# Lightning attention, LayerNorm and MLP on one core: 64-token chunks for two more pairs, block products for two more groups, and a newly written order of the steady part

## The chip, the cores and the metric

The kernel runs on one core of one Trainium2 chip. A core has a matrix engine (TensorE, PE in the profile; its weight loads are a row of their own, PEld), a vector engine (VectorE, DVE), an activation engine (ScalarE, ACT), a general engine (GpSimd, POOL) and a sync engine (SyncE, SP) that here only issues DMAs. The engines run side by side and wait for each other on semaphores. The metric is device time in microseconds (us) of one execution.

## The reference

Inputs are q, k and v of shape (4 batches, 8 heads, 768 tokens, 64), a decay `lam` per head, a gain of 512 and two weight matrices (512 x 2048 and 2048 x 512), all float32. The core of what is computed:

```python
for b in range(nb):                       # 12 blocks of 64 tokens, one after the other
    qb, kb, vb = q[:, :, sl], k[:, :, sl], v[:, :, sl]
    intra = (qb @ kb^T) * Dmask           # Dmask[i,j] = lam^(i-j) for i >= j, else 0
    intra = intra @ vb
    inter = (qb * lam^(pos+1)) @ kv_state
    out[:, :, sl] = intra + inter
    kv_state = lam^64 * kv_state + (kb * lam^(63-pos))^T @ vb
x = out as (4, 768, 512)                  # heads side by side
mu, var = mean and variance of x over the last axis
xn = (x - mu) / sqrt(var + 1e-6) * g_ln
result = x + maximum(xn @ w_ch1, 0) @ w_ch2
```

The state makes one sequence of a batch sequential; a chunk of 128 tokens in place of 64 gives the same result with other decays.

## The kernel before

**Tiling.** The work is cut into 12 pairs u = 0 to 11. A pair is 256 tokens of one batch (u counts batches first, then the three stretches of 256 tokens), that is two tiles of 128 tokens. Each pair goes through: load of k, q and v (256 tokens x 8 heads x 64 each, 512 KB); casts to bf16 with the decay folded into q and v (`in_k`, `in_q`, `in_v`, on GpSimd, VectorE or ScalarE); a transposition of k and q into `kqT` (on TensorE for pairs 0 to 2, by two DMAs, `transpose_dma` in L253, for pairs 3 to 10, by one for pair 11); scores, mask, scores times v (`av`), the state's update (`kv`, `new_state`) and its contribution (`inter`); then LayerNorm (`norm`, `rstd_of`), a transposition of the normalised rows into `xT` (`to_xT`, on TensorE for pairs 0 to 4, by two DMAs for the others), layer 1 of the MLP with a relu into `hT`, and layer 2, with the residual added as the accumulators are emptied.

**Two forms of attention.** Pairs u < LB = 6 work in chunks of 128 tokens: `scores` (L266) makes 128-wide products, `av` (L427) takes 64 small matmuls. Pairs from LB on work in chunks of 64: `scores64` (L361), `av64` (L416, 32 matmuls), `kv64`, and `states64`, which forms two states per tile on VectorE and GpSimd. The form also decides the shape of the loads: `fill` (L72) fetches a tensor of a pair below LB in one DMA whose rows are 512 bytes, and of a pair from LB on in two DMAs with rows of 256 bytes.

**Two forms of layer 2.** Groups g are pairs again. Groups 0 to 3 use the dense form `m2` (L667): per tile 16 matmuls of 128x512 into one accumulator. Groups 4 to 11 use seven block products (`product`, `m2w`): the hidden and output dimensions are halved, operand sums of `hT` are formed on VectorE (`h_sums`, L557), combinations of the weights are formed once (`w_sums`, L802), and each product is 8 matmuls of 128x256. Its seven results are scaled and added up by `evict` (L587) on VectorE, ScalarE and GpSimd.

**What sets the order.** Nothing is scheduled: every engine runs its instructions in the order in which the Python code issues them. The steady part is a hand-written list of statements; `units(n)` issues the next n pieces of MLP work from a second list, `plan`, and functions such as `X(u)` and `s12(u)` issue several attention steps. All loads of k, q and v, all DMA transpositions and all stores stand in one queue, SP's, in the order of the list; the loads of w1 and w2 stand in GpSimd's. The input buffers are three deep per tensor, accumulators for MLP work four (tag mm), for attention's output one per tile (po0, po1), for scores two (sc).

Of the kernel before, what the change touches and what calls it, by code (L numbers as in the profile page):

```python
# [17 lines left out]
def kernel(  # L18
# [436 lines left out]
    def reader(u):  # L455
        s = st[u]
        for ab in range(2):
            if s["S"][ab][1] is not None:
# [53 lines left out]

    def rstd_of(u):
        s = st[u]
        std = wk.tile([128, 2], F32, tag="std", name="std")
        if "sum" in s:
            ss = xp.tile([128, 2], F32, tag="ss", name="ss")
            for ab in range(2):
                sq = wk.tile([128, DM], BF16, tag="sq", bufs=1, name="sq")
                nc.scalar.activation(sq, s["x"][:, ab], ACT.Square, bias=s["nmean"][:, ab:ab + 1], accum_out=ss[:, ab:ab + 1])  # L520
            nc.scalar.activation(std, ss, ACT.Sqrt, bias=eps_t, scale=XS * XS / DM)
# [869 lines left out]
```

## Time and profile before

| | before |
|---|---|
| median of 3 runs | 207.53 us (207.52 to 208.06) |
| span of the profiled execution (first to last instruction) | 205.7 us |
| TensorE busy | 195.9 us, 95% |
| VectorE busy | 133.4 us, 65% |
| ScalarE busy | 122.0 us, 59% |
| GpSimd busy | 83.9 us, 41% |
| moved by DMA | 36.41 MB in 91011 packets |
| layer 1 matmuls (L547), 640 | 73.9 us busy |
| dense layer 2 matmuls (L684), 128 | 29.8 us busy |

The profile is that of one execution. A row of the page's fifth part, or of the view that groups instructions, reads: line of the kernel, engine, operation, output<-input by the program's names, shape, count | busy time in us, mean of one in ns | idle time of the engine ahead of them and what ended it. In the chain of waits each row has a start, a duration and a group of instructions. A row of SP's queue gives the start of an issue and the time until the queue was free for the next one; when the transfer itself has landed is told by the view of DMA issues. Durations of single matmuls overlap (a mean of 273 ns stands beside a rate of one in 109 ns), so rates are taken from the chain.

### The profile page before, as it was taken

The page shows a single profiled execution, that of the slowest core. Times are in us where ns is not written, and L with a number is a line of the kernel's source. Part 1 is how long each engine was busy: PE and PEld are TensorE (multiplying, and loading weights), DVE is VectorE, ACT ScalarE, POOL GpSimd, SP SyncE. Part 2 cuts the span into 40 slices and gives each one's busy share as a digit, 9 for nine tenths or more (in the row PEclk, how much of TensorE's full clock was granted, in tenths as well). Part 3 has the DMA queues.
Part 4 walks back from the last instruction along what each step waited for, and adds up shares of the span by engine and source line. Part 5 has one row for each costly group of instructions (what it writes and reads, how often), then busy time and mean ns, then how long its engine had stood idle before and what let it go on. Part 6 is the DMA issues. An engine that isn't in the chain of part 4 may idle for free.

```text
span 205.7 us, 7488 instructions
## 1 busy us (share of the span) xinstructions
PE 195.9 (95%) x3223; PEld 157.8 (77%) x3223; DVE 133.4 (65%) x277; ACT 122.0 (59%) x281; POOL 83.9 (41%) x117
## 2 busy tenths in 40 slices
PE   1997999999999999999999999999999999999992
PEld 0485798545784686489889888888888888988881
DVE  3588352626766458777889774857877947865253
ACT  3787678535357468166575775585586565652630
POOL 5557039317656341464273261772273202002020
PEclk9999999999999999999999999999999999999999
DMA  3999999999899998999799999887988020178404
GB/s 105 301 255 203 179 281 192 198 293 277 194 268 252 217 183 190 170 256 213 165 201 134 220 213 135 207 169 128 234 133 183 4 51 3 26 131 273 139 7 97
DMA packets 91011, 36.41 MB, mean 177 GB/s; under 512 B 65121, under 2 KB 88161, under 8 KB 90978
## 3 DMA queue, kind: packets, MB, share of 16 engines
q1 hardware_dynamic: 86368, 31.53, 74.9%
q0 software_dynamic: 4224, 4.19, 12.7%
q8 instruction: 25, 0.41, 0.9%
q10 hardware_dynamic: 386, 0.20, 0.4%
q14 instruction: 8, 0.07, 0.1%
HBM read 27.27 MB, written 6.29 MB: 163 GB/s over the span
## 4 chain that ended last, share of the span: by engine, by line
PE 85%; DMA 6%; DVE 2%; ACT 2%; SPq 1%; issue 1%; POOL 0%; POOLq 0%; DVEq 0%
PE pm L547 34%; PE pm L684 14%; PE pm1t L658 6%; PE pwd L582 6%; PE pwa L582 6%; PE pwc L582 6%; DMA w<-in_moe_w_ch_dram 4%; PE pwb L582 3%; DMA qin<-in_q_dram 3%; PE po L449 2%; PE po L436 2%; DVE x L595 1%; PE po L423 1%; PE sc L370 1%; PE sc L279 1%; PE pk L324 1%
## 5 line engine op out<-in xcount | busy, mean ns | idle before, releaser
L547 PE MATMUL pm<-xT,w 128*128 128x256 bf16 x640 | 73.9, 273 | 0.4 <-DMA w<-in_moe_w_ch_dram 0.4
L547 PEld LDWEIGHTS <-w 128*128 128x128 bf16 x640 | 61.2, 98 | 8.7 <-DMA w<-in_moe_w_ch_dram 0.5
L550 ACT ACTIVATE hT<-pm 128x512 f16<-128x512 f32 x80 | 47.1, 597 | 28.7 <-PE pm L547 28.5
L684 PE MATMUL pm<-w,hT 128*128 128x512 f16 x128 | 29.8, 380 | 0.0
L582 PEld LDWEIGHTS <-hs 128*128 128x128 f16 x256 | 24.9, 98 | 2.9
L607 POOL TENSOR_TENSOR x<-ev_u,x 128x256 f32<-128x256 f32 x8 | 5.9, 743 | 48.8 <-ACT ev_u L606 37.4
L330 POOL TENSOR_TENSOR Sn<-Stmp,lam_s 128x256 bf16<-128x256 f32 x16 | 9.8, 616 | 33.0 <-DVE Stmp L408 17.9
L565 DVE TENSOR_TENSOR hs<-hT 128x1024 f16<-128x1024 f16 x16 | 12.7, 795 | 15.8 <-ACT hT L550 14.5
L684 PEld LDWEIGHTS <-hT 128*128 128x128 f16 x128 | 11.8, 98 | 12.4
L582 PEld LDWEIGHTS <-hT 128*128 128x128 f16 x192 | 18.7, 98 | 2.1
L658 PE MATMUL pm1t<-xT,w 128*128 128x128 bf16 x256 | 15.6, 219 | 1.0 <-DMA w<-in_moe_w_ch_dram 0.7
L477 DVE SCALAR_TENSOR_TENSOR xc<-po,nmean,g_row 128x512 bf16<-128x512 f32 x18 | 13.0, 745 | 5.0 <-ACT nmean L476 4.9
L658 PEld LDWEIGHTS <-w 128*128 128x128 bf16 x256 | 14.8, 98 | 1.5 <-DMA w<-in_moe_w_ch_dram 0.8
L475 ACT ACTIVATE x<-po 128x512 f32<-128x512 f32 x18 | 10.6, 590 | 7.8 <-PE po L449 4.5
L242 POOL TENSOR_TENSOR vb<-vin,lam_v 128x1024 bf16<-128x1024 f32 (+1 forms) x7 | 11.6, 1659 | 4.8 <-DMA vin<-in_v_dram 4.7
L520 ACT ACTIVATE sq<-x,nmean 128x512 bf16<-128x512 f32 x18 | 12.9, 719 | 0.3
L242 POOL TENSOR_TENSOR vb<-vin,lam_p 128x1024 bf16<-128x1024 f32 x6 | 11.4, 1896 | 3.1 <-ACT hT L550 1.9
L289 DVE TENSOR_TENSOR mA<-sc,keep 128x512 bf16<-128x512 f32 x14 | 9.0, 682 | 4.9 <-PE sc L279 4.9
L661 ACT ACTIVATE hT<-pm1t 128x512 f16<-128x512 f32 x16 | 9.6, 598 | 4.4 <-PE pm1t L658 4.3
L595 DVE SCALAR_TENSOR_TENSOR x<-pwd,rstd,x 128x256 f32<-128x256 f32 x16 | 7.7, 481 | 3.4 <-POOL x L615 3.4
L595 DVE SCALAR_TENSOR_TENSOR x<-pwa,rstd,x 128x512 f32<-128x512 f32 (+1 forms) x16 | 9.1, 612 | 0.8
L582 PE MATMUL pwa<-w,hT 128*128 128x256 f16 x64 | 9.6, 273 | 0.0
(137 smaller groups left out, 318.0 us busy)
## 6 DMA issues: line engine op xcount, KB each, us to landing
out_dram<-x SPq DMA_DIRECT2D x22, 256.0 KB, 4.0
w<-in_moe_w_ch_dram POOLq DMA_DIRECT2D x8, 512.0 KB, 8.0
kin<-in_k_dram SPq DMA_DIRECT2D x14, 256.0 KB, 5.2
qin<-in_q_dram SPq DMA_DIRECT2D x14, 256.0 KB, 4.2
vin<-in_v_dram SPq DMA_DIRECT2D x14, 256.0 KB, 5.3
kin<-in_k_dram SPq DMA_DIRECT2D x5, 512.0 KB, 6.2
qin<-in_q_dram SPq DMA_DIRECT2D x5, 512.0 KB, 7.0
vin<-in_v_dram SPq DMA_DIRECT2D x5, 512.0 KB, 6.1
```

The costliest lines, as they stand in the source:

```text
L242: eng.tensor_tensor(st[u]["vb"][:, hs], qkv_in[u]["v"][:, hs], lv.to_broadcast([128, n, 2, D]), op=ALU.mult)
L330: eng.tensor_tensor(dst, src, lam_s[:, :, None].to_broadcast([128, NP, D]), op=ALU.mult)
L475: nc.scalar.activation(x, po, ACT.Copy, accum_out=sm)
L477: nc.vector.scalar_tensor_tensor(xc, in0=po, scalar=nm, in1=g_row, op0=ALU.add, op1=ALU.mult)
L520: nc.scalar.activation(sq, s["x"][:, ab], ACT.Square, bias=s["nmean"][:, ab:ab + 1], accum_out=ss[:, ab:ab + 1])
L547: nc.tensor.matmul(pm[:, b, :], lhsT=w1[n // W2K][:, kk, (n % W2K) * 128:(n % W2K + 1) * 128], rhs=xT_of[g][:, kk, 0:N], start=(b == 0 and ...
L550: nc.scalar.activation(hT[:, u * NB:(u + 1) * NB, 0:N], pm, ACT.Relu)
L565: nc.vector.tensor_tensor(s13, b[:, :, 1:2, :].to_broadcast([128, n, 2, 128]), b[:, :, 0:4:3, :], op=ALU.subtract)
L582: nc.tensor.matmul(pr[bank], lhsT=lhs(r), rhs=rhs, start=(first and r == 0), stop=(r == KB // 2 - 1), skip_group_check=True)
L595: nc.vector.scalar_tensor_tensor(out, in0=in0, scalar=r[ab], in1=in1, op0=ALU.mult, op1=ALU.add)
L658: nc.tensor.matmul(pm[:, b, :], lhsT=w1[c][:, kk, b * 128:(b + 1) * 128], rhs=xT_of[g][:, kk, i * 128:(i + 1) * 128], start=(b == 0 and kk ...
L684: nc.tensor.matmul(acc[i], lhsT=hT[:, kk, i * 128:(i + 1) * 128], rhs=w2[kk // W2K][:, kk % W2K, :], start=(kk == 0), stop=(kk == KB - 1))
```

## The change

There are four parts.

1. `LB` goes from 6 to 4: pairs 4 and 5 use 64-token chunks. Their k, q and v are therefore loaded in two DMAs each.
2. `WG` is gone: all groups from 2 on use block products, so groups 2 and 3 change form.
3. Some steps are split so that their halves can stand apart: `states64` into `sums64` (VectorE) and `pools64` (GpSimd), the last step of `norm` becomes `center`, the squares of `rstd_of` become `squares`, `wind_up` loses `wind_down`. `kv64` may use the po accumulators, and `reader` is told its engine.
4. The steady part, from the transpositions of pair 2 on, is a flat list of single statements in a new order. The opening is as before.

The core of the diff ("..." where lines are left out):

```diff
-    WG = 4
-    LB = 6
+    LB = 4
...
-    def kv64(u):
+    def kv64(u, tag="mm"):
         s = st[u]
         last = (u // B + 1) * W >= S
-        s["pk"] = [mm_tile([128, 2, NP, D], F32, f"pk{ab}") for ab in range(2)]
+        s["pk"] = [ps.tile([128, 2, NP, D], F32, tag=f"po{ab}" if tag == "po" else tag, bufs=dict(mm=4, sc=2, po=1)[tag],
+                           name=f"pk{ab}") for ab in range(2)]
...
-            decay(nc.gpsimd, Sn, tmp)
+    def pools64(u, j):
+        s = st[u]
+        b = u % B
+        if s["tmp"] is not None:
             Sn = wk.tile([128, NP, D], BF16, tag="S", bufs=12, name="Sn")
+            decay(nc.gpsimd, Sn, s["tmp"])
...
-        if g >= WG:
-            plan += [(m2.w, n) for n in range(8)]
-        else:
-            plan += [(m2, i, part) for i in range(len(groups[g])) for part in range(KB // 4)]
...
+    open_in(3, True)
+    open_in(4, False)
+    new_state(1, 1, nc.gpsimd)
     transpose_pe(2, 0, (0, 1, 2, 3), nc.vector)
+    load_in(3, "q", nc.sync)
...
+    load_in(3, "k", nc.sync)
...
+    load_in(3, "v", nc.sync)
...
+    in_q_one(4, nc.gpsimd, 0)
+    w_sums(3, 0)
+    m2a(1, 2)
     in_k_one(3, nc.vector, 1)
+    w_sums(2, 1)
     transpose_dma(3, 0)
     transpose_dma(3, 1)
+    in_k_one(4, nc.gpsimd, 0)
+    m2b(0, 2)
+    in_v(3, nc.gpsimd)
...
     load_in(4, "v", nc.sync)
+    load_in(5, "v", nc.sync)
+    center(2, 1)
     load_in(5, "k", nc.sync)
+    m2a(0, 3)
     to_xT(2, 0)
+    in_k_one(4, nc.gpsimd, 1)
+    transpose_dma(4, 0)
+    m2a(1, 3)
     load_in(5, "q", nc.sync)
+    in_q_one(4, nc.gpsimd, 1)
     to_xT(2, 1)
+    m2b(1, 2)
+    m2b(1, 3)
+    m1g[2](0)
+    m1g[2](1)
+    kv(3, "po")
+    scores(3, 1)
+    scores(3, 0, early=True)
...
+    m2s[2].w(4)
+    to_xT(3, 1)
+    m2s[2].w(5)
+    scores64(4)
+    squares(3, 0)
+    kv64(4, "po")
...
+    transpose_dma(7, 0)
+    mask64(6, 1)
+    m1g[4].tile(2, 1)
+    m1g[4].tile(3, 0)
+    m1g[4].tile(3, 1)
+    squares(5, 0)
+    load_in(8, "q", nc.sync)
...
+    m2s[4].w(5)
+    transpose_dma(7, 1)
...
+    scores64(7)
```

What the order does to SP's queue around the transposes of pair 4. Before, where kq_1214 is pair 4 and kin_1177, qin_1178, vin_1179 are the inputs of pair 5, kin_1537 that of pair 6:

```order
L257 DMA_TRANSPOSE kqT_1165<-kq_1047 128x8x128 x2
L76 DMA vin_908<-in_v_dram 128x8x128
L76 DMA kin_1177<-in_k_dram 128x8x128
L76 DMA qin_1178<-in_q_dram 128x8x128
L257 DMA_TRANSPOSE kqT_1220<-kq_1214 128x8x128 x2
L76 DMA vin_1179<-in_v_dram 128x8x128
L716 DMA out_0_dram<-x_390 64x2x512 x2
L80 DMA kin_1537<-in_k_dram 128x8x64 x2
```

After, where kq_959 is pair 4, vin_948, kin_946 and qin_947 are the inputs of pair 5, and kin_1137 that of pair 6:

```order
L256 DMA_TRANSPOSE kqT_1196<-kq_942 128x8x128 x2
L79 DMA vin_869<-in_v_dram 128x8x64 x2
L79 DMA vin_948<-in_v_dram 128x8x64 x2
L79 DMA kin_946<-in_k_dram 128x8x64 x2
L256 DMA_TRANSPOSE kqT_1251<-kq_959 128x8x128
L79 DMA qin_947<-in_q_dram 128x8x64 x2
L256 DMA_TRANSPOSE kqT_1251<-kq_959 128x8x128
L79 DMA kin_1137<-in_k_dram 128x8x64 x2
```

The load of v of pair 5 now stands ahead of both transposes of pair 4, and the load of q of pair 5 between the two.

SP's queue around the transposes of pair 7 (kq_1697 before, kq_1829 after; x_704 and x_1137 are rows of pairs 1 and 2 that are stored). Before, with qin_1917 and vin_1918 the inputs of pair 8:

```order
L80 DMA vin_1582<-in_v_dram 128x8x64 x2
L80 DMA kin_1916<-in_k_dram 128x8x64 x2
L716 DMA out_0_dram<-x_704 64x2x512 x2
L716 DMA out_0_dram<-x_1137 64x2x512 x2
L503 DMA_TRANSPOSE xT_2357<-xc_2279 128x4x128
L257 DMA_TRANSPOSE kqT_2359<-kq_1697 128x8x128 x2
L503 DMA_TRANSPOSE xT_2357<-xc_2279 128x4x128
L80 DMA qin_1917<-in_q_dram 128x8x64 x2
L80 DMA vin_1918<-in_v_dram 128x8x64 x2
```

After, with kin_2111, vin_2113 and qin_2112 the inputs of pair 8 and x_1147 the rows of pair 2:

```order
L256 DMA_TRANSPOSE kqT_2114<-kq_1162 128x8x128 x2
L79 DMA kin_2111<-in_k_dram 128x8x64 x2
L79 DMA vin_2113<-in_v_dram 128x8x64 x2
L731 DMA out_0_dram<-x_1147 64x2x512 x2
L515 DMA_TRANSPOSE xT_2342<-xc_2324 128x4x128
L256 DMA_TRANSPOSE kqT_2363<-kq_1829 128x8x128
L79 DMA qin_2112<-in_q_dram 128x8x64 x2
L256 DMA_TRANSPOSE kqT_2363<-kq_1829 128x8x128
L515 DMA_TRANSPOSE xT_2342<-xc_2324 128x4x128
```

The loads of v and q of pair 8 stand ahead of pair 7's second transpose where they stood behind it, and the store of pair 1 has gone further back.

GpSimd around the scaling of pair 3's v (vb_1048 before, vb_943 after). Before, with kq_1214 of pair 4:

```order
L231 CAST kq_1047<-kin_899 128x4x128
L236 TENSOR_TENSOR kq_1047<-qin_900,lam_q_143 128x4x128 x2
L242 TENSOR_TENSOR vb_1048<-vin_901,lam_v_145 128x1024
L231 CAST kq_1214<-kin_906 128x4x128 x2
L236 TENSOR_TENSOR kq_1214<-qin_907,lam_q_143 128x4x128 x2
```

After, with kq_959 of pair 4:

```order
L230 CAST kq_942<-kin_863 128x4x128
L235 TENSOR_TENSOR kq_959<-qin_868,lam_p_146 128x4x128
L230 CAST kq_959<-kin_867 128x4x128
L241 TENSOR_TENSOR vb_943<-vin_865,lam_v_145 128x1024
L230 CAST kq_959<-kin_867 128x4x128
```

One cast of q and one of k of pair 4 now stand ahead of pair 3's v.

More of the change, by code (lines that the diff above doesn't have):

```diff
@@ L515, in rstd_of @@
         std = wk.tile([128, 2], F32, tag="std", name="std")
[L516 to L521, printed above, removed]
+        if "ss" in s:
+            nc.scalar.activation(std, s["ss"], ACT.Sqrt, bias=eps_t, scale=XS * XS / DM)
         else:
@@ L1095 @@
-    s4(2)
+    m1b(5)
+    m1b(6)
+    scores(2, 0)
+    open_window(3)
+    in_q_one(3, nc.gpsimd, 1)
+    load_in(3, "k", nc.sync)
+    open_in(5, False)
+    m1b(7)
+    open_window(4)
+    open_window(5)
+    in_q_one(3, nc.gpsimd, 0)
+    mask(2, 0)
+    m2b(0, 0)
+    load_in(3, "v", nc.sync)
+    new_state(0, 1, nc.gpsimd)
+    scores(2, 1)
+    kv(2, "po")
+    new_state(2, 0, nc.gpsimd)
+    new_state(2, 1, nc.gpsimd)
+    m2a(0, 0)
+    m2a(1, 0)
+    mask(2, 1)
+    m2a(0, 1)
+    m2b(0, 1)
@@ new lines @@
+    load_in(8, "k", nc.sync)
+    load_in(8, "v", nc.sync)
+    in_q_one(7, nc.gpsimd, 0)
+    sums64(6, 0)
+    pools64(6, 0)
+    sums64(6, 1)
+    in_k_one(7, nc.vector, 1)
+    av64(5)
+    inter(5, 0, fence=False)
+    reader(5, nc.scalar.copy)
+    in_v(7, nc.gpsimd)
+    m1g[4](1)
+    m1g[4](2)
+    open_window(8)
+    scores64(6)
+    store(2)
+    in_k_one(8, nc.gpsimd, 0)
+    inter(5, 1)
+    norm(5, 0)
+    m1g[4](3)
+    center(5, 0)
+    norm(5, 1)
+    to_xT(5, 0)
+    m1g[4].tile(2, 0)
@@ new lines @@
+    squares(6, 0)
+    m1g[5].tile(2, 1)
+    in_k_one(8, nc.vector, 1)
+    m1g[5].tile(3, 0)
+    in_v(8, nc.gpsimd)
+    m2s[5].sums(0, 4)
+    in_q_one(8, nc.gpsimd, 1)
+    m1g[5].tile(3, 1)
+    m2s[5].w(0)
+    load_in(9, "q", nc.sync)
+    m2s[5].w(1)
+    m2s[5].sums(4, 8)
+    m2s[5].w(2)
+    in_q_one(9, nc.gpsimd, 0)
+    m2s[5].w(3)
+    m2s[5].w(4)
+    to_xT(6, 0)
+    squares(6, 1)
+    in_q_one(9, nc.gpsimd, 1)
+    m2s[5].w(5)
+    in_k_one(9, nc.scalar, 1)
+    to_xT(6, 1)
+    m1g[6](0)
@@ new lines @@
+    in_q_one(11, nc.gpsimd, 0)
+    transpose_dma(10, 1)
+    scores64(10)
+    mask64(10, 0)
+    kv64(10)
+    to_xT(8, 1)
+    squares(8, 1)
+    store(3)
+    mask64(10, 1)
+    load_in(11, "v", nc.sync)
+    m1g[8](0)
+    center(9, 0)
+    sums64(10, 0)
+    in_q_one(11, nc.gpsimd, 1)
+    m1g[8](1)
+    m1g[8](2)
+    norm(9, 1)
+    to_xT(9, 0)
+    m1g[8](3)
+    center(9, 1)
+    rstd_of(8)
+    m2s[8].sums(0, 4)
+    m1g[8](4)
+    m1g[8](5)
+    m1g[8](6)
+    m1g[8](7)
+    pools64(10, 0)
@@ new lines @@
+    scores64(11)
+    reader(10, nc.scalar.copy)
+    kv64(11)
+    inter(10, 1)
+    norm(10, 0)
+    sums64(11, 0)
+    pools64(11, 0)
+    center(10, 0)
+    sums64(11, 1)
+    norm(10, 1)
+    m1g[9](2)
+    squares(9, 1)
+    m1g[9](3)
+    center(10, 1)
+    m1g[9](4)
+    rstd_of(9)
+    m2s[9].sums(0, 4)
+    m1g[9](5)
+    m1g[9](6)
+    m1g[9](7)
+    m2s[9].sums(4, 8)
+    m2s[9].w(0)
+    m2s[9].w(1)
+    squares(10, 0)
+    m2s[9].w(2)
+    m2s[9].w(3)
+    squares(10, 1)
+    m2s[9].w(4)
@@ L1364 @@
+    m2s[10].w(4)
+    to_xT(11, 1)
+    m2s[10].w(5)
+    m2s[10].w(6)
+    m2s[10].w(7)
+    m1g[11](0)
+    m1g[11](1)
+    m1g[11](2)
+    m1g[11](3)
+    m2s[11].sums(0, 4)
+    store(9)
+    m1g[11](4)
+    m1g[11](5)
+    m1g[11](6)
+    m1g[11](7)
+    m2s[11].sums(4, 8)
+    store(10)
+    m2s[11].w(0)
+    m2s[11].w(1)
+    store(6)
+    m2s[11].w(2)
+    m2s[11].w(3)
+    m2s[11].w(4)
+    m2s[11].w(5)
+    m2s[11].w(6)
+    m2s[11].w(7)
 _INS = ['q', 'k', 'v', 'lam', 'moe_g_ln', 'moe_w_ch1', 'moe_w_ch2']
```

713 lines of the change are left out of this document (334 added, 379 removed).

## The prediction, made before the changed kernel was run

> **What bounds the kernel now.** I read the page's engine shares first, then its chain of waits, then the busy time by stage. The first two rows:
>
> ```profile
> PE 195.9 (95%) x3223; PEld 157.8 (77%) x3223; DVE 133.4 (65%) x277; ACT 122.0 (59%) x281; POOL 83.9 (41%) x117
> PE 85%; DMA 6%; DVE 2%; ACT 2%; SPq 1%; issue 1%; POOL 0%; POOLq 0%; DVEq 0%
> ```
>
> An average of 95% can hide a stage in which TensorE waits, so the busy time of each engine in stretches (columns: PE, PEld, DVE, ACT, POOL, clock, DMA share, GB/s):
>
> ```profile
> 55.00:60.00 5.00, 5.00 (x103) 4.31 (x102) 3.85 (x9) 2.93 (x5) 1.90 (x1) 1.00 1.16 297
> 60.00:95.00 35.00, 35.00 (x715) 24.49 (x714) 23.86 (x50) 20.92 (x53) 17.39 (x20) 1.00 1.14 216
> 95.00:100.00 5.00, 5.00 (x58) 4.58 (x56) 3.16 (x7) 2.90 (x7) 1.44 (x2) 1.00 1.04 138
> 140.00:160.00 20.00, 20.00 (x294) 17.84 (x292) 15.67 (x30) 13.24 (x33) 8.30 (x10) 1.00 0.88 166
> 160.00:180.00 20.00, 20.00 (x351) 17.69 (x349) 14.56 (x32) 12.66 (x29) 2.80 (x5) 1.00 0.10 21
> 201.70:205.70 4.00, 0.13 (x2) 0.00 (x0) 0.65 (x2) 0.00 (x0) 0.00 (x0) 1.00 0.41 98
> ```
>
> Two things are to be seen. TensorE is busy for the whole of every stretch of the steady part, at a granted clock of 1.00, so there is no idle time to win; a reordering can gain only what it takes off TensorE. And the DMA engines are full too: a share over 1 until 100 us, still 0.88 at 160, then almost nothing. So up to some 100 us a second resource stands as full as TensorE, and the kernel runs at TensorE's pace only because each transfer lands a little before it is read. How little is the question of this prediction.
>
> **What leaves TensorE.** From the chain of waits (start, duration, group), whose durations already leave out the overlap of pipelined matmuls:
>
> ```profile
> 67.15 1.73 PE pm L684 x8
> 68.88 0.38 PE pk L324 x32
> 69.70 0.97 PE pm L684 x4
> 73.29 0.64 PE po L436 x64
> 90.14 0.38 PE sc L370 x32
> 97.82 0.87 PE pwc L582 x8
> 101.42 0.37 PE po L423 x32
> 102.43 0.28 PE sc L370 x32
> ```
>
> Layer 2 of a group has 32 dense matmuls, so 32 x 1.73/8 = 6.92 us; as seven block products it has 56, so 56 x 0.87/8 = 6.09. Two groups: -1.66 us. Attention times values is 64 small matmuls at 0.64 for a 128-token pair and 32 at 0.37 for a 64-token pair: 2 x 0.27 = -0.54. The scores of a 128-token pair lie between the end of its pk group, 69.26, and the next dense group at 69.70, so 0.44; those of a 64-token pair take 0.28 to 0.38: I take 2 x 0.15 = -0.30, bounds -0.1 and -0.3. Against that, a group of big matmuls right behind small ones is slower (0.97 for four, 0.865 by the first row), and the new list cuts TensorE's work into 24 runs of small matmuls where there were 19: 5 x 0.1 = +0.5, bounds 0 and +0.7, the upper end with the short gap ahead of such a group counted too. Sum -2.0 us, between -1.8 and -2.5. The profiled span is 205.7 and the median of the runs 207.53: some 1.8 us lie around the span, and I leave them as they are. Were nothing else touched, the time would be **205.5 us**.
>
> **What is added to the other engines.** The products of groups 2 and 3 need operand sums and more evictions on VectorE:
>
> ```profile
> L565 DVE TENSOR_TENSOR hs<-hT 128x1024 f16<-128x1024 f16 x16 | 12.7, 795 | 15.8 <-ACT hT L550 14.5 <-ACT hT L661 1.3
> L566 DVE TENSOR_TENSOR hs<-hs,hT 128x512 f16<-128x512 f16 x16 | 8.7, 543 | 0.6
> L567 DVE TENSOR_TENSOR hs<-hs,hT 128x512 f16<-128x512 f16 x16 | 6.8, 425 | 0.5
> L708 DVE SCALAR_TENSOR_TENSOR x<-pm,rstd,x 128x512 f32<-128x512 f32 x8 | 5.8, 741 | 2.6 <-PE pm L684 2.6
> ```
>
> The three kinds of sums occur twice each per group (16 in the eight groups that have them): 2 x (0.795 + 0.543 + 0.425) = 3.5 us. Evictions: two of 0.741 become six, of which half are half as wide, some +1.6 per group. Together some +10 us for the two groups, while two pairs lose two of four masks. They fall mostly between 60 and 95, where VectorE is busy for 23.86 of 35 us, and the weight combinations that stand there now go ahead of 60. That makes about 30 of 35: full, though not over. I cost it at nothing in the sum, with the work of TensorE as cover; where the cover fails, at most one eviction or mask at a time is late, 0.7 us, and three such places would eat the gain. That is a rival below.
>
> On GpSimd, the scaling of pair 3's v moves behind the first cast of pair 4's k, and so behind that load. Before:
>
> ```profile
> 45.71 0.61 POOL L231 CAST kq<-kin 128x512 bf16<-128x512 f32 x1 [4.55 <-DMA kin<-in_k_dram]
> 49.44 1.90 POOL L242 TENSOR_TENSOR vb<-vin,lam_v 128x1024 bf16<-128x1024 f32 x1
> kin<-in_k_dram SPq DMA_DIRECT2D x1, 512.0 KB, 7.6
> ```
>
> The last row is the load of pair 4's k, issued at 43.66: it landed at 51.3. It now stands behind pair 4's q, about 2 us later: 53.3, plus 0.61 for the cast and 1.90 for the scaling gives 55.8. Pair 3's state products, which read that result, come on TensorE at about 55.1 by the chain's durations in the new order. So 0.7 us late, bounds 0 and 1.
>
> **What is added to the DMA queue, and what it does to the transposes.** SP's queue in order of time (start, time until the next can be issued, line):
>
> ```profile
> 43.66 1.70 SPq L76 DMA_DIRECT2D kin<-in_k_dram  x1
> 45.47 1.63 SPq L76 DMA_DIRECT2D qin<-in_q_dram  x1
> 55.53 5.16 SPq L257 DMA_TRANSPOSE kqT<-kq  x2
> 69.29 2.03 SPq L80 DMA_DIRECT2D vin<-in_v_dram  x2
> 83.91 2.15 SPq L80 DMA_DIRECT2D vin<-in_v_dram  x2
> 86.11 1.93 SPq L80 DMA_DIRECT2D kin<-in_k_dram  x2
> 88.08 3.57 SPq L716 DMA_DIRECT2D out_dram<-x  x4
> 92.55 1.22 SPq L503 DMA_TRANSPOSE xT<-xc  x1
> 93.88 2.77 SPq L257 DMA_TRANSPOSE kqT<-kq  x2
> ```
>
> A tensor in one DMA of 512-byte rows takes 1.63 to 1.70; in two of 256-byte rows (the form that pairs 4 and 5 now get) 1.93 to 2.15. That is +0.4 for each of six tensors, +2.4 in all. The queue has hardly a hole, so a load that is put ahead of a transpose delays it by its full price. [...]
>
> Now the landings. For the transposes of pair 4 (second one) and pair 7 (second one), the view of the tile, or of the DMA issues, in a window around them has:
>
> ```profile
> L257 SPq DMA_TRANSPOSE kqT<-kq x1: 1711/1711/1711, 59.0 to 59.0; - x1
> DMA to landing us min/median/max: 5.2/5.2/5.2
> kqT<-kq SPq DMA_TRANSPOSE x1, 4.4
> ```
>
> Pair 4: issued at 59.0, landed at 64.2, and read by its scores at about 69.1, so 4.9 us early. In the new list its scores come at 67.1 (fewer matmuls ahead of them). Ahead of the transpose now stand v of pair 5 (2.1; it was behind it), and five tensors of pairs 4 and 5 in short rows (5 x 0.4 = 2.0): 64.2 + 4.1 = 68.3, so 1.2 us late; it is also split from its partner by a load, for which I take nothing and hold 1.2 as upper bound.
>
> Pair 7: the second was issued at 95.2 (the pair starts at 93.88) and landed at 99.6, against scores at 102.4 by the chain. In the new list these come at about 100.3. Ahead of it are now all six short-row tensors (2.4), v of pair 8 and q of pair 8 (2.1 each, both behind it before), and one store less (half of 3.57, -1.8). Of the hole before 92.55 (88.08 + 3.57 = 91.65) 0.9 is won back, since more is ready to issue. 99.6 + 2.4 + 4.2 - 1.8 - 0.9 = 103.5: 3.2 us late, between 0 (if the queue drains faster with more in flight) and 5.3 (each of the two split pairs 0.6 to 1.2 more). Transposes of pairs 5 and 6 lie between these two. From pair 8 on the new list has about the same work ahead of each transpose as the old one, and the share falls to 0.88 and 0.10, so nothing new is late there.
>
> TensorE works in order, so it stands still until the transpose is there, and what is lost isn't won back, since it is busy throughout afterwards. Each lateness is counted against the unshifted schedule, so the largest one decides, not their sum. With 0.5 for what the short waits on GpSimd and VectorE add where they don't fall together, the loss is 3.2 + 0.5 = 3.7 us.
>
> **Forecast:** 207.53 - 2.0 + 3.7 = **209.2 us**, slower, the DMA queue setting TensorE's pace between about 55 and 105 us; its own range 207.7 to 211.0.
>
> **The rivals.**
>
> A. Everything lands in time, and only TensorE's work counts: 205.5. For it: the slack that I use up is a difference of sums of some 100 us of queue time, and 256-byte rows in a deeper queue may cost less than the row-by-row spacing shows; loads issued early also fill holes such as the one at 91.65. It decides if the second transpose of pair 7 lands by 100.5. Against it: a DMA share above 1 in every stretch up to 100 us.
>
> B. The transposes are on time but short waits (pair 3's v at 0.7, two or three late VectorE results of 0.7 each where it is 30 of 35 us busy) cost about what TensorE gains: 207.5, between 206.7 and 208.2.
>
> C. The queue is worse than I count: both upper bounds, 5.3 at pair 7 and the 1.0 on GpSimd: 207.53 - 2.0 + 6.3 = 211.8. For it: a pair of transposes split by a load occurs for pairs 4 and 7, and in the row at 55.53 even an unsplit pair held the queue for 5.16.
>
> [...]
>
> **How the numbers follow.** Forecast 0.44, A 0.29, B 0.15, C 0.10, D 0.02. A measurement of this kernel tells 0.3%, 0.62 us, from no change: below 206.9 is faster, above 208.15 slower. Faster: A and a small part of B and of the forecast's low end, 0.32. Same: most of B and the low edge of the forecast, 0.15. Slower: the rest, 0.53. Cases of both signs are likely, so the range reaches from A to near C, 205.1 to 211.5, and leaves out D, most of C and the tail of A, under 2 in 10.
>
> **What would show it.** Right: TensorE's idle time in the new profile is some 4 us more than now, all before about 105 us, the releaser of the scores (of pairs 4 to 7) is a DMA of kqT, and SP's row of the second transpose of pair 7 starts near 99. TensorE's busy time drops by about 2 whatever else happens; if it drops by less than 1.5 the first sum is wrong. Wrong: scores that find their kqT there, with TensorE at 5.00 of 5.00 in all stretches (A), or idle time in front of TensorE ended by VectorE or GpSimd (B). If idle time appears behind 110 us, my claim that the later transposes keep their slack has failed.

## The result, and the profile after

The changed kernel takes 214.36 us in the median of four runs (212.84 to 215.86), against 207.53 before: a ratio of 1.0315, interval 1.0257 to 1.0374. It is slower, as forecast, but 5.2 us beyond the forecast and outside the range. The profiled execution is the one of 212.84 us, so what follows accounts for 212.84; the 1.5 us from there to the median no trace shows. In what follows a median is of all executions of a kernel, its fastest and slowest stand in brackets, and no ratio is given for two kernels of which all executions but one count as slow, being over 1.5% above the fastest.

The first page has these shares of the engines and of the chain of waits:

```profile
PE 196.7 (93%) x3207; PEld 162.9 (77%) x3207; DVE 139.9 (66%) x297; ACT 122.1 (58%) x285; POOL 88.0 (42%) x125
PE 73%; DMA 12%; ACT 4%; DVE 3%; POOL 3%; issue 2%; SPq 1%; POOLq 0%; DVEq 0%; ACTq 0%
```

TensorE's share of the chain falls from 85 to 73%, the DMA's doubles from 6 to 12%. Yet TensorE is busy for 0.8 us more than before, where two us less was expected. The busy time by stage (PE, PEld, DVE, ACT, POOL, clock, DMA share, GB/s) says where:

```profile
60.00:85.00 25.00, 23.63 (x414) 20.42 (x412) 18.90 (x39) 14.97 (x36) 12.73 (x18) 1.00 1.07 207
85.00:100.00 15.00, 14.00 (x315) 12.39 (x314) 12.35 (x24) 10.84 (x28) 9.26 (x12) 1.00 1.10 191
100.00:105.00 5.00, 3.58 (x46) 2.87 (x44) 2.99 (x6) 2.09 (x9) 2.02 (x3) 1.00 1.25 203
105.00:110.00 5.00, 3.86 (x81) 2.98 (x81) 3.29 (x7) 0.60 (x1) 2.52 (x3) 0.73 1.04 218
110.00:140.00 30.00, 30.00 (x519) 26.69 (x518) 18.50 (x39) 18.60 (x49) 12.27 (x18) 0.99 0.88 155
```

TensorE stands still between 60 and 110 for 1.37 + 1.00 + 1.42 + 1.14 = 4.9 us, nowhere after it, and in the stretch from 105 to 110 the granted clock is 0.73, where it was 1.00 before. What it stood for, from the view of waits of TensorE and its timeline (the bracket is the idle time ahead of the row and what ended it):

```profile
PE sc L369 <- DMA kqT<-kq: 3.9, 4, 1.8
PE pm L562 <- DMA xT<-xc: 0.8, 1, 0.8
PE pm L562 <- DVE x L610: 0.2, 1, 0.2
```

```profile
68.06 0.44 PE L369 MATMUL sc<-kqT 64*64 64x64 bf16 x32 [0.78 <-DMA kqT<-kq]
...
83.02 0.45 PE L369 MATMUL sc<-kqT 64*64 64x64 bf16 x32 [0.37 <-DMA kqT<-kq]
...
91.17 0.44 PE L369 MATMUL sc<-kqT 64*64 64x64 bf16 x32 [0.99 <-DMA kqT<-kq]
...
105.34 0.45 PE L369 MATMUL sc<-kqT 64*64 64x64 bf16 x32 [1.76 <-DMA kqT<-kq]
...
106.84 5.32 PE L562 MATMUL pm<-xT,w 128*128 128x256 bf16 x32 [0.80 <-DMA xT<-xc]
```

These are the scores of pairs 4, 5, 6 and 7, each waiting for the second half of its own transpose, and then layer 1 of the next group, waiting for the transpose of x. The last row shows more: its 32 matmuls take 5.32 us. In the kernel before, the chain of waits has the same group in two rows, which take 3.7 us together; the chain after follows:

```profile
103.74 0.89 PE pm L547 x8
...
104.64 2.79 PE pm L547 x24
```

```profile
102.36 4.35 DMA xT<-xc
...
106.84 5.32 PE pm L562 x32
```

So 1.6 us went into matmuls that ran slowly right behind the longest wait. The clock says about the same: at 0.73 over the five microseconds from 105 and 0.66 over the one from 110, 5 x 0.27 + 0.34 = 1.7 us are missing. On SP's queue (start, time until the next) the second transpose of pair 7 starts at 100.60; it started at 95.2 before:

```profile
98.11 1.96 SPq L79 DMA_DIRECT2D qin<-in_q_dram  x2
...
100.60 1.65 SPq L256 DMA_TRANSPOSE kqT<-kq  x1
```

The account of the span: 205.7 before, + 4.9 idle from 60 to 110, + 1.7 slow clock, - 0.9 that TensorE's work really became shorter (busy 196.7 - 1.7 against 195.9), - 0.3 of idle time elsewhere: 211.1.

### The profile page after: what moved, and what is told of

It is laid out like the page before. It is cut to its first block, busy times and chain, and to the rows that moved or that the text cites. A ratio compares the mean times of both kernels' runs of the same rounds, so it can differ in the third digit from the quotient of the medians.

```text
span 211.1 us, 7499 instructions
## 1 busy us (share of the span) xinstructions
PE 196.7 (93%) x3207; PEld 162.9 (77%) x3207; DVE 139.9 (66%) x297; ACT 122.1 (58%) x285; POOL 88.0 (42%) x125
## 4 chain that ended last, share of the span: by engine, by line
PE 73%; DMA 12%; ACT 4%; DVE 3%; POOL 3%; issue 2%; SPq 1%; POOLq 0%; DVEq 0%; ACTq 0%
PE pm L562 31%; PE pm L699 7%; PE pwa L597 6%; PE pm1t L673 6%; PE pwc L597 6%; PE pwd L597 5%; DMA w<-in_moe_w_ch_dram 3%; PE pwb L597 3%; DMA qin<-in_q_dram 3%; DMA xT<-xc 2%; DVE x L610 2%; DMA lam_b<-in_lam_dram 2%; DMA kqT<-kq 1%; PE po L456 1%; PE tp L249 1%
## 5 line engine op out<-in xcount | busy, mean ns | idle before, releaser
L562 PE MATMUL pm<-xT,w 128*128 128x256 bf16 x640 | 76.6, 277 | 1.3 <-DMA xT<-xc 0.8
L597 PEld LDWEIGHTS <-hs 128*128 128x128 f16 x320 | 31.1, 98 | 3.6
L597 PEld LDWEIGHTS <-hT 128*128 128x128 f16 x240 | 23.0, 98 | 2.7
L241 POOL TENSOR_TENSOR vb<-vin,lam_p 128x1024 bf16<-128x1024 f32 x8 | 15.2, 1896 | 1.5 <-DMA vin<-in_v_dram 1.5
L235 POOL TENSOR_TENSOR kq<-qin,lam_p 128x512 bf16<-128x512 f32 x13 | 13.7, 1056 | 3.7 <-DMA qin<-in_q_dram 3.7
L699 PE MATMUL pm<-w,hT 128*128 128x512 f16 x64 | 14.9, 380 | 0.0
L610 DVE SCALAR_TENSOR_TENSOR x<-pwa,rstd,x 128x512 f32<-128x512 f32 (+1 forms) x20 | 11.4, 612 | 1.0 <-PE pwa L597 0.4
L597 PE MATMUL pwa<-w,hT 128*128 128x256 f16 x80 | 12.0, 273 | 0.0
L597 PE MATMUL pwb<-w,hT 128*128 128x256 f16 x80 | 11.5, 273 | 0.0
L230 POOL CAST kq<-kin 128x512 bf16<-128x512 f32 x9 | 6.6, 735 | 10.7 <-DMA kin<-in_k_dram 10.6
```

Of the source, the lines that this page charges most:

```text
L235: eng.tensor_tensor(part(1, st[u]["kq"], ALL)[:, :, :, j], src[:, :, :, j], lq[:, :, :, None].to_broadcast([128, NP, 2, D]), op=ALU.mult)
L241: eng.tensor_tensor(st[u]["vb"][:, hs], qkv_in[u]["v"][:, hs], lv.to_broadcast([128, n, 2, D]), op=ALU.mult)
L562: nc.tensor.matmul(pm[:, b, :], lhsT=w1[n // W2K][:, kk, (n % W2K) * 128:(n % W2K + 1) * 128], rhs=xT_of[g][:, kk, 0:N], start=(b == 0 and ...
L597: nc.tensor.matmul(pr[bank], lhsT=lhs(r), rhs=rhs, start=(first and r == 0), stop=(r == KB // 2 - 1), skip_group_check=True)
L610: nc.vector.scalar_tensor_tensor(out, in0=in0, scalar=r[ab], in1=in1, op0=ALU.mult, op1=ALU.add)
L699: nc.tensor.matmul(acc[i], lhsT=hT[:, kk, i * 128:(i + 1) * 128], rhs=w2[kk // W2K][:, kk % W2K, :], start=(kk == 0), stop=(kk == KB - 1))
```

## The experiments

In the code "..." stands for lines left out; the comments in them are added here.

**Are the loads put ahead of the transposes the cause?** In the changed kernel the loads of pairs 5, 7 and 8 that the new order pulls ahead of a transpose go back behind it, with the casts that read them:

```diff
-    load_in(5, "v", nc.sync)      # and q of 5: ahead of the transposes of pair 4
-    load_in(7, "k", nc.sync)      # ahead of those of pair 5
-    load_in(7, "v", nc.sync)      # ahead of those of pair 6
-    load_in(8, "v", nc.sync)      # and q of 8: ahead of those of pair 7
...
+    load_in(8, "q", nc.sync)      # behind the transpose of x, as before
+    load_in(8, "v", nc.sync)
```

> The changed kernel, with the loads of q and v of pair 5, k and v of pair 7, q and v of pair 8 put back behind the DMA transposes that they were pulled ahead of (and the GpSimd and ScalarE steps that read them moved behind their neighbours). Theory (the transposes are late because of the loads ahead of them, and TensorE's clock falls because it waits for them): the idle time of TensorE between 60 and 110 us falls from 4.9 us to under 1.5, the granted clock is 1.00 throughout, and the time is 205.5 to 208. Rival (short rows make the queue too slow wherever the loads stand): idle time stays at 2.5 us or more, time 210 or more. Rival (the time is lost in the fuller VectorE and GpSimd): idle time before TensorE is ended by these two, time above 210.

210.82 us (210.36 to 212.39), ratio 1.0179 (1.0138 to 1.0221), clock 0.999. Waits of TensorE, and one row of GpSimd:

```profile
PE po L456 <- POOL Sm L420: 1.8, 1, 1.8
PE pm L562 <- DMA xT<-xc: 1.0, 1, 1.0
PE xt L522 <- DVE xc L499: 0.7, 1, 0.7
PE sc L369 <- DMA kqT<-kq: 0.7, 2, 0.4
```

```profile
94.45 0.73 POOL L230 CAST kq<-kin 128x512 bf16<-128x512 f32 x1 [4.82 <-DMA kin<-in_k_dram]
```

The waits for the transposes shrink from 3.9 to 0.7 us, those of pairs 4 to 7 are gone (the two that are left stand at 134 and 150 us), and the clock stays up: that far the theory holds. But the median gives back only 3.5 us. TensorE still stands for 2.6 us between 60 and 110, where under 1.5 was expected, and GpSimd and VectorE end these waits, as the last rival had it. Pair 7's v, moved back, now stands ahead of pair 8's k in SP's queue; GpSimd waits 4.82 us for that k and starts its cast at 94.45, where it started at 92.95 in the changed kernel. The state that TensorE needs next is queued behind that cast, and TensorE waits 1.8 us for it. The lateness changed its place.

**What does a load ahead of a transpose cost by itself?** In the kernel before, the loads of pair 8's q and v go ahead of the transpose of pair 7, and nothing else is touched; in a second kernel only q:

```diff
+    load_in(8, "q", nc.sync)
+    load_in(8, "v", nc.sync)      # left out in the second kernel
     transpose_dma(7, 0)
...
-    load_in(8, "q", nc.sync)
-    load_in(8, "v", nc.sync)
```

> The kernel before, with one edit: the loads of q and v of pair 8 stand ahead of the two transposes of pair 7, where they stood behind them. No short rows, no other change of order. Theory (two loads of about 2.1 us against a slack of 2.8 us): pair 7's second transpose lands 3.5 to 4.5 us later, at 103 to 104, TensorE waits 0.7 to 1.7 us for it and about as long for the normalised rows of pair 5 that come behind, and the median is 208.3 to 210.5. Rival (loads only fill holes of the queue): landing stays within 1.5 us of 99.6, no wait, median 207.2 to 207.8.

> The kernel before with only the load of q of pair 8 ahead of pair 7's transposes (half of the edit that cost 6.7 us). Theory (landing moves by about 3 us a load, as it moved by 6.4 for two, against a slack of 2.8): the second transpose lands at 102 to 103.3, TensorE waits 0 to 1 us, the clock stays at 1.00, median 207.5 to 209. Rival (any load ahead of the transposes already upsets the queue's order): landing at 104 or later, clock falls, median 210 or more.

Two loads: 214.2 us (213.34 to 214.83), ratio 1.0296 (1.0249 to 1.0343). One load: 207.97 (207.31 to 210.26), ratio 1.001 (0.9968 to 1.0053). SP's queue, the landing of the second transpose in the chain of waits, TensorE's timeline and one-microsecond stretches with two loads:

```profile
94.18 1.21 SPq L80 DMA_DIRECT2D qin<-in_q_dram  x2
95.43 3.88 SPq L80 DMA_DIRECT2D vin<-in_v_dram  x2
99.44 3.20 SPq L257 DMA_TRANSPOSE kqT<-kq  x2
```

```profile
101.39 4.84 DMA kqT<-kq
```

```profile
106.28 0.64 PE L370 MATMUL sc<-kqT 64*64 64x64 bf16 x32 [3.82 <-DMA kqT<-kq]
```

```profile
104.00:105.00 1.00, 0.00 (x0) 0.00 (x0) 0.00 (x0) 0.00 (x0) 0.50 (x2) 1.00 0.75 134
105.00:106.00 1.00, 0.00 (x0) 0.00 (x0) 0.00 (x0) 0.00 (x0) 0.00 (x0) 0.72 0.72 16
106.00:107.00 1.00, 0.72 (x48) 0.72 (x47) 0.03 (x1) 0.00 (x0) 0.00 (x0) 0.50 0.47 108
111.00:112.00 1.00, 1.00 (x7) 0.69 (x6) 0.00 (x0) 0.09 (x1) 1.00 (x2) 0.50 0.02 2
```

and with one load the same scores:

```profile
102.39 0.45 PE L370 MATMUL sc<-kqT 64*64 64x64 bf16 x32 [0.32 <-DMA kqT<-kq]
```

Two moved loads alone cost nearly as much as the whole change, and more than the theory said. The pair of transposes is issued 5.6 us later (99.44 against 93.88), and the second lands at 106.2 instead of 99.6: 6.6 us for two loads, 3.3 each, not the 2.1 of a queue row. One load uses up the slack (landing 102.35, a wait of 0.32) and is free, as its theory said. And with two the clock falls to 0.50 before the wait of 3.82 us is over (0.72 over 105 to 106) and stays there for 6.8 us in all (0.87 over 112 to 113), 0.8 of them in the wait, so that the profiled span grows by 6.6 us (205.7 to 212.3) and not by 3.8.

**Is the slow clock the wait's doing?** The wait is filled with matmuls whose result nobody reads, ahead of pair 7's scores, in the changed kernel and in the kernel with two loads moved:

```diff
+    fill_pe(24, "sc", True)       # after, ahead of scores64(7)
```
```diff
+        if u == 7:
+            fill_pe(60, "sc", True)   # before with two loads moved
```

> The changed kernel, with 24 matmuls of 128x128 that nobody reads put ahead of pair 7's scores, where TensorE stands still for 1.8 us. Theory (the clock falls to half for some 3.5 us because TensorE has been idle for most of the 3 us before): with the wait filled the granted clock stays at 1.00 between 107 and 111, layer 1's first 32 matmuls of group 5 take 3.5 us and not 5.3, and the time falls by 1.8 us, to about 211 to 212.5. Rival (the clock falls for another reason, such as the load or the time since the start): the clock still falls there, and the time stays at 213 to 216 or grows by the filler.

> The kernel before with the loads of q and v of pair 8 ahead of pair 7's transposes (the run before, 214.2), and 60 matmuls of 128x128 that nobody reads ahead of pair 7's scores, where TensorE stood still for 3.8 us. Theory (the wait costs its own 3.8 us and, through the clock at half for 7 us behind it, about 3 more): with TensorE kept busy the clock stays at 1.00, the transposes land as late as before, and the median is 210.8 to 212.2. Rival (the clock falls for another reason than the idle time, or the time behind the wait is lost to DMA): median 213.5 to 215 again.

The chain of each, first of the changed kernel with its wait filled:

```profile
106.52 3.65 PE pm L562 x32
```

then of the kernel before with two loads moved, unfilled and filled:

```profile
108.75 5.27 PE pm L547 x32
```

```profile
107.55 3.49 PE pm L547 x32
```

In both pairs the group behind the wait goes back from 5.3 to 3.5 or 3.65 us, and the clock of the profiled execution to 1.00; the second transpose lands within 0.5 us of where it did (105.8 against 105.3, and 106.1 against 106.2). So TensorE's standing still, and not something else at that place, takes the clock down. The profiled spans fall by 2.0 (211.1 to 209.1) and 1.6 (212.3 to 210.7). The medians say less: 212.66 (210.78 to 216.41), ratio 1.0255 (1.0176 to 1.0334), and 213.83 (212.08 to 215.99), ratio 1.0248 (1.0171 to 1.0325). Both lie above the range of their theory, the second in that of its rival, and both intervals overlap those of the unfilled kernels. The mean granted clock, which is on record for every execution, does tell them apart: it is 0.973 to 0.992 in the eight unfilled executions and 0.998 or more in six of the eight filled ones; the other two, at 0.983 and 0.992, are the slowest of their kernels. So that the filled wait keeps the clock up is shown; what it is worth in time, the traces alone show.

How much standing still is enough, the rows bound. The clock fell after waits of 1.76 and 0.80 us with 0.70 us of matmuls between them, and in the last of the orders tried below (mean clock 0.992) at waits of 0.97 and 1.83 with 0.6 between, where six matmuls of 128x256 take 1.46 us and six in the kernel with products for both groups (mean clock 1.00) 0.82. In the changed kernel with long rows (below) the longest wait is 2.4, and the mean clock of the execution 0.987. It did not fall after one wait of 1.8 us (loads moved back, mean clock 0.999) or 2.01 (loads back and long rows, 0.999), nor after 1.40 and 0.81 us with 1.45 between (short rows alone, 0.998). So 2.56 us in two pieces sufficed, and by the mean clock 2.4 in one, where 2.21 in two and 2.01 in one did not; where between them the limit lies, and what sets it, no run shows. Where it is lowest the clock stands at 0.50, in the changed kernel from 108 to 110 us, with two loads from 106 to 108 and still at 111; the shares of the windows put the whole of it at some 3.4 and 6.8 us.

**What do the short rows cost?** In the kernel before, the six tensors of pairs 4 and 5 are loaded as two DMAs of 256-byte rows, at their old places; and the changed kernel with rows of 512 bytes for these pairs, which mixes up their tokens and leaves everything else:

```diff
+        if u < LB and u >= 4:
+            for j in range(2):
+                eng.dma_start(got[:, hs, j * D:(j + 1) * D], ...)   # every second token
+            return
```
```diff
-        if u < LB:
+        if u < 6:
```

> The kernel before, with only the loads of pairs 4 and 5 changed: two DMAs of 256-byte rows in place of one of 512-byte rows, six tensors, the same bytes to the same places. Theory (0.4 us more per tensor, and a slack of 4.9 us at pair 4 and 2.8 at pair 7): the second transpose of pair 4 lands about 1.5 to 2 us later than 64.2 and that of pair 7 up to 2.4 later than 99.6; TensorE still never waits; time 207.5, within 0.3%. Rival (short rows cost twice as much): transposes of pair 7 come too late, TensorE waits 2 us or more, and the time is 210 or more.

> The changed kernel in its order, with the loads of pairs 4 and 5 as one DMA of 512-byte rows each; the tokens of these two pairs then lie in another order than the attention takes them to be in, so what it computes for pairs 4 and 5 is not the reference's, with the same work. Theory (loads ahead of transposes cost more than the short rows: 4.2 us of loads against 2.4 of rows at pair 7): idle time falls from 4.9 us by about 2, and with it perhaps the slow clock; time 209 to 212.5. Rival (the short rows are the cause): idle time under 1 us, clock 1.00, time 206 to 207.5. Rival (rows cost nothing): 213 to 216.

Short rows alone: 211.31 us (209.98 to 214.1), ratio 1.0168 (1.0112 to 1.0224). SP's queue and the waits of TensorE:

```profile
98.82 3.01 SPq L262 DMA_TRANSPOSE kqT<-kq  x2
```

```profile
PE sc L375 <- DMA kqT<-kq: 1.4, 1, 1.4
PE pm L552 <- DMA xT<-xc: 0.8, 1, 0.8
```

The transposes of pair 7 start at 98.82 instead of 93.88, 4.9 us later with six tensors ahead. By the end of TensorE's wait, at 103.9, the second lands some 4.2 us later, 0.7 a tensor; at pair 4, with five ahead, it lands 2.6 later (66.8 against 64.2), 0.5 a tensor. That is more than the 0.4 of the prediction, and it is enough to end the slack by itself; I had expected no difference, and the time lies where the rival had it. A single row of the queue is no measure of this price: in the kernel before, a long-row tensor holds the queue for anything from 0.57 to 1.70 us between 43 and 61 us, and here pair 4's k and q hold it for 3.47 and 2.80 us where it was 1.70 and 1.63, about twice as long.

Long rows in the changed kernel: 210.48 us (206.53 to 213.18, the other two 209.97 and 210.98). Its profiled execution is the slowest, and still has

```profile
PE sc L369 <- DMA kqT<-kq: 3.1, 2, 2.4
```

so the new order makes the transposes late without the short rows too; between 60 and 110 TensorE stands for 3.4 us, of 4.9. The median lies in the range of the theory, but four executions that are 6.7 us apart decide little. The one at 206.53 is below all eight of the kernel before that ran beside it (207.09 to 208.31); it wasn't traced, so what made it fast stays open.

**Both together.** Loads moved back and long rows:

> The changed kernel with both undone: the loads behind the transposes, as in the first experiment, and long rows for pairs 4 and 5 (their tokens lie in another order than the attention takes them to be in, so the result of these pairs is not the reference's, with the same work). With the other three kernels this makes two by two. Theory (the waits on transposes come from loads ahead and short rows together): no wait on kqT over 0.5 us, clock 1.00; what idle time is left comes from VectorE and GpSimd, under 2.5 us; median 206.5 to 209. Rival (something else in the new order makes transposes late): waits on kqT of 1.5 us or more, median over 210.

211.07 us (208.7 to 211.44), ratio 1.0117 (1.0049 to 1.0185).

```profile
PE sc L369 <- DMA kqT<-kq: 2.6, 3, 2.0
```

```profile
135.12 0.45 PE L369 MATMUL sc<-kqT 64*64 64x64 bf16 x32 [2.01 <-DMA kqT<-kq]
```

This is what the rival said, though at another place: the wait is now at 135 us, at pair 9. By the medians, either repair alone gives back 3.5 to 3.9 us of the 6.8, and both together no more than one.

**Can the order be mended?** Two tries: the changed kernel with all loads back and in addition pair 3's q behind its k, and pair 8's k, the store of pair 2 and pair 9's q each behind the next transpose, with their casts; and the kernel before with short rows and the two stores ahead of pair 7's transposes put behind them:

```diff
+    load_in(8, "k", nc.sync)      # behind the transpose of x; likewise store(2)
...
+    load_in(9, "q", nc.sync)      # behind the next one
```
```diff
-    store(1)
-    store(2)
     transpose_dma(7, 0)
...
+    store(1)
+    store(2)
```

> The changed kernel with all loads put back behind the transposes that were ready (those of the first experiment, and also q of pair 3 behind the loads of w2, k of pair 8 and the store of pair 2 behind pair 7's transposes, q of pair 9 behind the normalised rows of pair 6), and the GpSimd casts that read them moved behind the state work that must not wait. Theory (what the change loses is transposes and GpSimd steps that stand behind loads): idle time of TensorE between 60 and 120 us under 1.5 us, granted clock 1.00 throughout, median 205.5 to 207.5, with a spread of the runs as small as that of the kernel before (about 1 us). Rival (six short-row tensors alone make the queue too slow by some 2 us at pair 7, whatever the order): waits of scores or layer 1 on DMAs of 1.5 us or more, median 208.5 to 210.

> The kernel of the short-row run (the kernel before with 256-byte rows for pairs 4 and 5, 211.3 us), with the stores of pairs 1 and 2 moved from ahead of pair 7's transposes to behind them and the rows of pair 5. Theory (lateness is a sum over what stands ahead in SP's queue, whatever it is: the stores are 3.4 us there, the second transpose landed about 1.4 too late): it lands at 99.5 to 102, TensorE does not wait for it or under 0.3 us, and the median is 207.3 to 208.8. Rival (short rows slow the queue down in itself, so that what stands behind them is late whatever is moved): waits of 1 us or more for pair 7 or later, median 210 or more.

The theory missed in both, and the waits that the rivals name are there. The first: 213.24 us (212.52 to 213.72), ratio 1.026 (1.0213 to 1.0308), clock 1.00:

```profile
PE pm L562 <- DVE x L610: 2.1, 2, 1.2
PE sc L369 <- DMA kqT<-kq: 2.0, 2, 1.5
PE pm L562 <- DMA w<-in_moe_w_ch_dram: 1.6, 1, 1.6
```

```profile
122.29 0.45 PE L369 MATMUL sc<-kqT 64*64 64x64 bf16 x32 [1.48 <-DMA kqT<-kq]
```

The second: 214.83 us (210.46 to 216.88), the profiled execution 214.92:

```profile
136.02 0.45 PE L375 MATMUL sc<-kqT 64*64 64x64 bf16 x32 [0.97 <-DMA kqT<-kq]
138.43 1.46 PE L552 MATMUL pm<-xT,w 128*128 128x256 bf16 x6 [1.83 <-DVE xc L482]
```

Pair 7 has no wait any more in either, which is what moving the transfers was for; pair 8 (at 122 us) or pair 9 (at 136) has one, and VectorE ends waits that are as long or longer (2.1 us in two pieces in the first, 1.8 in the second). That a transfer moved back hands its lateness on to a later transpose fits these two kernels, but no run shows that it is the same lateness.

**Do the block products pay by themselves?** In the kernel before, groups 2 and 3, and then group 3 alone, get layer 2 as seven products, with the weight sums made early and the scores of the pairs there split so that the sums fit between:

```diff
-        if g >= WG:
+        if g >= 2:                # second kernel: 3
...
+    w_sums(2, 0)                  # ahead of 70 us
+    m2s[3].sums(0, 4)
```

> The kernel before with one part of the change: layer 2 of groups 2 and 3 as seven block products. The loads keep their long rows and their order, pairs 4 and 5 their 128-token chunks; the weight combinations are formed earlier, and the second half of the scores of pairs 4 and 5 comes one or two pieces of MLP work later, since the products hold four accumulators. Theory (the change's gain is real and is lost to late transposes): TensorE does 1.7 us less, waits at most 0.5 us for VectorE, no wait on DMA, and the median is 205.5 to 207.0. Rival (block products gain nothing, since their sums and evictions on VectorE come late where groups 2 and 3 stand): waits on VectorE of 1.5 us or more between 60 and 92 us, median 207.5 to 209.

> The kernel before with layer 2 of group 3 alone as block products (half of that part of the change), the weight combinations moved to where VectorE was half idle (62 to 70 us), the two halves of pair 5's scores two pieces of MLP work apart. Loads as before. Theory (a group as block products saves TensorE 0.83 us, and the 5 us that it adds to VectorE fit between 76 and 92 us): no wait of TensorE over 0.5 us, median 206.5 to 207.3 against 207.6. Rival (VectorE, already 82% busy there, comes late): waits on VectorE of 1 us or more around 80 to 95 us, median 207.8 to 210.

Both groups: 215.85 us (215.11 to 217.74), ratio 1.0389 (1.0337 to 1.0442). Group 3: 210.44 (209.94 to 210.59), ratio 1.0106 (1.0061 to 1.0152). The theory missed in both; the rivals name the cause, waits on VectorE, and put it too low. With both groups, a stretch and the two largest rows of TensorE's waits in the steady part:

```profile
65.00:70.00 5.00, 3.11 (x35) 2.64 (x33) 4.90 (x7) 2.65 (x10) 5.00 (x4) 1.00 1.21 292
```

```profile
PE pm L547 <- DVE x L708: 2.4, 2, 1.4
PE po L449 <- DVE seen L460: 1.9, 1, 1.9
```

The 2.4 us stand at 55 and 58 us, ahead of the first block product (64.4): VectorE forms the weight combinations there, moved forward in this kernel, and its evictions of a dense group come late. The 1.9 us stand at 67, in the stretch shown. In it VectorE is busy for 4.90 of 5 us and GpSimd for all 5, yet VectorE has only seven instructions there. With group 3 alone the timeline shows a case of it:

```profile
66.37 2.19 POOL L242 TENSOR_TENSOR vb<-vin,lam_v 128x1024 bf16<-128x1024 f32 x1 [2.07 <-DMA vin<-in_v_dram]
...
66.83 2.01 DVE L811 TENSOR_TENSOR wt<-w,wt 128x512 f16<-128x512 f16 x1
...
70.66 0.42 DVE L811 TENSOR_TENSOR wt<-w,wt 128x512 f16<-128x512 f16 x1
```

The same sum takes 0.42 us alone and 2.01 beside a scaling of v on GpSimd: that ends at 68.56, and the sum 0.3 later. It takes 1.6 us more, where 1.7 us of GpSimd's operation were left when it began; what in the two holds it up no run shows. So VectorE's time has to be counted with GpSimd's beside it. How much of the waits comes from this, and how much from where the weight combinations were put, no run took apart.

On TensorE itself the products do gain, though less than worked out. Each matmul counted from its start to that of the next (at most its own length), in us:

```
                        before   after   group 3   both groups
layer 2                  78.0     76.9     77.5       77.2
scores                    5.7      5.2      6.0        6.4
av and q times state     10.6     10.7     11.2       10.9
all matmuls             195.9    196.7    196.9      197.2
```

(The 196.7 contain the 1.7 us of slow clock.) Layer 2 falls by 0.5 for one group and 0.8 to 1.1 for two; in the two kernels with products alone the small matmuls, cut into more and shorter runs, give as much back.

## Why the prediction was right or wrong

**The bound.** Right: before the change TensorE and the DMA queue are both full up to 100 us, and what the change does to the queue outweighs what it does for TensorE.

**The place and the mechanism.** Right: TensorE waits for kqT at pairs 4 to 7, all before 107 us (about 105 was said), and nothing is late behind that in the changed kernel. The rivals A (everything lands) and B (idle time ended by VectorE or GpSimd) are out for this kernel. So is the last one, D (217, given 0.02), for which each of the six tensors had to take twice its time, 1.66 us more: no run shows that price for all six, which moved pair 7's landing by 4.2 us and not by 10, though two rows of the queue did double (3.47 and 2.80 us for 1.70 and 1.63). C (211.8) came nearest, for other reasons: the idle time was 4.9 us and not its 6.3. B's mechanism is real, though: with the products alone, waits on VectorE are 5.5 of the 7.7 us by which the profiled span is longer (213.4 against 205.7).

**TensorE's work, "-2.0, between -1.8 and -2.5".** Wrong, by 1.1: its work fell by 0.9, less than the 1.5 below which the prediction calls its own sum wrong. Layer 2 gave 1.1 instead of 1.66, since the products go at 62.7/560 = 0.112 us each over all groups and not at the 0.109 of one long run; the scores gave 0.5 (0.3 expected); and attention times values together with q times the state rose by 0.1 where -0.54 stood: the first fell by 0.3, and the second, cut into more runs, rose by 0.4. The other matmuls rose by 0.6 together. Another 0.3 came from less idle time elsewhere. The bound of -1.8 is a slip besides: its own terms give -1.66 - 0.54 - 0.1 + 0.7 = -1.6.

**VectorE's +10 us at nothing.** Right in this kernel, where waits on VectorE and GpSimd come to 0.2 us; VectorE's busy time rose by 6.5 us and not by 10 (139.9 against 133.4), and pair 3's v, put at 0.7 late, was not waited for. Perhaps this is so only because the DMA held TensorE up at the same places: with the loads moved back such waits come to 2.5, with the products alone to 2.0 and 5.5. Those kernels have other orders, though, so that is argued and not shown.

**The short rows, "+0.4 for each of six tensors".** The size was wrong: 0.5 at pair 4 and 0.7 at pair 7. The rows of the queue from which it was taken, a few among many that differ, give the time until the next DMA can be issued, and the landing was later by more than that. With 0.7 for 0.4, the sum for pair 7's landing becomes 103.5 + 6 x 0.3 = 105.3, and it landed at 105.3 (100.60 + 4.7). That match flatters the sum: the loads ahead were too cheap as well, 3.3 each by the run with two loads where 2.1 stood, and by both prices it would be 107.7. What gave 2.4 back, the runs don't separate. At pair 4 the forecast of 68.3 came out (68.0), but that is luck: with 2.6 for the five tensors and 3.3 for the load the sum would be 70.1. Neither landing moved by the sum of the single prices.

**"The largest lateness decides".** Right in form: the waits up to pair 7 add up to 0.22 + 0.78 + 0.37 + 0.99 + 1.76 = 4.1, which is the lateness of the last one against the unshifted schedule; 3.2 was forecast. What was left out is the transpose of x right behind it, 0.8 later still. Idle time in all 4.9 against 3.7.

**The step that failed** is the price of a stall. It was put at the length of the wait, with the clock taken as 1.00 throughout, as the profile before has it. A clock that hadn't dropped in that profile said nothing on what it does behind a wait. It cost 1.7 us in the profiled execution here and 2.8 (6.6 - 3.8) in the kernel with two loads moved. It is the largest of the terms that were off, and without it the profiled execution would lie at 211.1, inside the range.

The terms together: forecast 209.2, + 1.1 - 0.3 on TensorE, + 1.2 idle, + 1.7 clock, and 0.1 less around the span, gives 212.8, the profiled run. The median lies 1.5 above it. Runs of one kernel with late transposes lie up to 6.7 us apart, those of the kernel before up to 3.5 (207.11 to 210.59), which would fit lateness and clock drops that differ from run to run. The mean clock of each run bears out a part: the slowest run of the changed kernel has 0.973 where the profiled one has 0.988, some 3.2 us of its 214, and is 3.1 us longer; the two between have 0.988 and 0.992, so that their 1.4 and 1.6 us more are not the clock's. Of seven runs of the kernel before above 209.5 us, five have 0.988 to 0.992, where all those below 209 have 0.995 or more. Since one run of each is traced, the rest is argued and not shown.

**Open.** With loads back and long rows the kernel is still 1.2% slower than before, some 2.4 us; the trace names waits on kqT at pair 9, on VectorE and on ScalarE, but no run took these apart. No kernel tried here beats the one before.

## What to carry to other kernels

When the DMA queue and TensorE are both full, keep a ledger for each transfer that TensorE reads: what is issued ahead of it, and by how much it lands early; a transfer moved ahead is free up to that slack (one load here) and costs its landing shift after it (about 3 us for 0.5 MB here, more than its row in the queue). Price a wait on TensorE as the wait and the slow matmuls behind it, where the clock falls: here it did after 2.56 us in two pieces close together and, by the mean clock of 0.987, with one of 2.4. Before moving work to an engine with idle time, look at what runs beside it: on VectorE a sum of 0.42 us took 2.0 beside GpSimd.

## What the runs showed of the hardware

- The granted clock went to 0.50 in the changed kernel, after TensorE stood for 2.56 us in two pieces, and stayed there for about 3.4 us (0.73 over 105 to 110 and 0.66 in the microsecond after); with two loads moved it went there 3.0 us into a wait of 3.82 and stayed for 6.8 us. With long rows, where the longest wait is 2.4 us, the mean clock is 0.987. Filling the wait with 24 or 60 unread matmuls kept it at 1.00 in the traced executions.
- Tensors in rows of 256 bytes moved landings by 0.5 to 0.7 us each against rows of 512 where the queue is full, 4.2 us for six.
- A load of 0.5 MB put ahead of a transpose moved its landing by 2.7 us, two by 6.6.
- A VectorE operation of 0.42 us, a sum in f16 or a cast to bf16, took 1.6 to 2.0 us beside GpSimd's scaling of v; not every one did, a sum that began together with the scaling, at 66.38 in the group 3 kernel, took 0.42. In the changed kernel, too:

```profile
90.80 1.64 DVE L230 CAST kq<-kin 128x512 bf16<-128x512 f32 x1
```

```profile
90.27 1.90 POOL L241 TENSOR_TENSOR vb<-vin,lam_p 128x1024 bf16<-128x1024 f32 x1
```
